# Row maxima in the softmax of a Linformer attention that feeds a SwiGLU block

## The chip, the cores and the metric

The kernel runs on 1 core of one Trainium2 chip. The metric is the device time of one execution in microseconds (us). Engines are named as in the profile: PE is TensorE's matmul, PEld its weight load, DVE is VectorE, ACT is ScalarE, POOL is GpSimd, SP is SyncE. Each engine works off its own queue in order; an instruction that waits holds up everything behind it on its engine.

## The reference

Attention with projected keys and values (8 batches, 8 heads, 1024 positions, head width 64, 64 projected positions), then a gated feed-forward block over the 8192 tokens (512 wide, 1536 hidden).

```
k_proj = einsum('ks,bhsd->bhkd', E, k);  v_proj = einsum('ks,bhsd->bhkd', F, v)
scores = (1/sqrt(64)) * q @ k_proj^T                  # rows of 64
scores = scores - max(scores, axis=-1)
attn = exp(scores);  attn = attn / (sum(attn, -1) + 1e-9)
x = attn @ v_proj, as 8192 x 512
out = (silu(x @ w_gate) * (x @ w_val)) @ w_out
```

## The kernel before

**Work and order.** The kernel is recorded in an order written out by hand; each engine executes its part of it in that order. The main loop runs over t = 0 to 191: 16 chunks c of 512 tokens (two to a batch) times 12 blocks f of 128 hidden columns. In step t, `f_g` puts four matmuls of 512 columns into a PSUM bank `gps`, and ACT takes the tanh of it into `th` (line 496). `f_v` does the same with the other weight into `vps`; DVE then forms `s1 = (th + 1) * g` (line 503) and `hT = 0.5 * s1 * v` (line 508). There are two `gps` and two `vps` banks, so the matmuls of step t+2 wait for the DVE instructions of step t. A PE that has nothing to wait for takes about 0.87 us for each set of four.

The second product of the block (with w_out) lags by one chunk. It is a Strassen-like form with seven products for each half of the chunk (`f_m`, six matmuls of 256 columns at a time, n = 0 to 13 over a chunk at f = 0, 1, 2, 3, 4, 4, 5, 6, 7, 8, 9, 10, 10, 11). ACT copies two of its PSUM results out (`xs`, line 603, at f = 1 and 7; `ysb`, line 610, at f = 3 and 9). The matmuls of n = 2 write the bank that the `xs` copy after n = 1 reads. For chunk 0 the plain form `f_y` is used, during steps 16 to 27.

**Attention.** It is fed in by slots; step t runs slot 2t between its `f_g` and its `f_v`, and slot 2t+1 at its end. A softmax unit u (8 to a batch, 64 in all) holds 128 rows of 8 score rows of 64: `u_S` makes four matmuls of 128 columns into a bank `sc`, and ACT takes one exponential over all 512 columns, with the scale 1/8 in it, into `ee` (line 357). `u_R`, one slot later, sums `ee` on DVE into `zz` (line 368, 128x8 from 128x512) and takes the reciprocals (line 370); `u_N` multiplies on POOL (line 383). For chunk 0 and 1 the result is turned by PE (`u_A`), for the others by a DMA on SP's queue (`u_AD`); `u_PV`, `u_PV1`, `u_PV2` or `u_PVt` multiply with the projected values and ACT or DVE copies the result into `xT`, which `f_g` and `f_v` read. `u_KV`, `u_K1` project keys and values, `u_KT`, `u_KT0` put the projected keys into the block matrix `BD`; ACT copies the keys out (lines 171 and 194). Score banks come from a ring: three banks while c < 2, two afterwards.

**Where the units stand.** Batch 0's units 0 to 3 (chunk 0) are computed before the loop, written out one call after the other (lines 776 to 819); there the first half of the tokens needs units 0 and 2, the second half units 1 and 3. Units 4 to 7 are in slots 13 to 16. The units of batch 1 are in slots 35 to 38 and 41 to 44, close together. Batch 2 has them in slots 48 + (17, 18, 22, 23, 27, 30, 33, 36), and each batch b from 3 on in slots 48(b-1) + (14, 17, 20, 23, 26, 29, 32, 35), one in three slots.

Of the kernel before, what the change touches and what calls it, by code (L numbers as in the profile page):

```python
# [10 lines left out]
ALU = mybir.AluOpType  # L11
# [27 lines left out]
def kernel(  # L39
# [110 lines left out]
    def copy(eng, out, in_):  # L150
        (nc.scalar.copy if eng is nc.scalar else eng.tensor_copy)(out=out, in_=in_)

    def u_KV(b, what="kv", hs=(0, H), at="a"):

# [15 lines left out]
        if "k" in what:  # L170
            nc.scalar.copy(out=ks[b % 2][0:64, h0:h1], in_=t[0:64, h0:h1])
        if "v" in what:
# [7 lines left out]
    def u_K1(b, gs=(0, 2), at="a"):  # L180
# [4 lines left out]
        for j in range(NJ):  # L185
            for c in range(2):
# [6 lines left out]
                )  # L193
        nc.scalar.copy(out=ksp[b][:, 2 * g0 : 2 * g1], in_=t[:])

# [115 lines left out]

    def u_T(b, u, at="a", eng=nc.scalar):
# [10 lines left out]
        t = first_batch("q", [P, 4, P], "qT")  # L323
        copy(eng, t[:], ps[:])
        qT[b, u] = t

# [15 lines left out]

    def u_S(b, u, at="a"):
        ch, w = divmod(u, 4)
# [6 lines left out]
        for n in range(4):  # L351
            slot = (0, 2, 1, 3)[n] if (b, ch) in BY_DMA else n
            nc.tensor.matmul(  # L353
                out=ps[:, slot, :], lhsT=t[:, n, :], rhs=BD[b % 2][:, 4 * g + n, :], start=True, stop=True
            )
        e = aw.tile([P, 4, 2, KP], FP32, name="ee", tag="ee", bufs=4)
        nc.scalar.activation(  # L357
            out=e[:].rearrange("p h j k -> p (h j k)"),
            in_=ps[:].rearrange("p a k -> p (a k)"),
            func=AF.Exp,  # L360
            scale=scale,
        )
        ee[b, u] = e

    def u_R(b, u):
        e = ee[b, u]
        z = aw.tile([P, 4, 2], FP32, name="zz", tag="zz", bufs=3)
        nc.vector.reduce_sum(out=z[:], in_=e[:], axis=AX.X)  # L368
        r = aw.tile([P, 4, 2], FP32, name="rr", tag="rr", bufs=4)
        nc.vector.reciprocal(out=r[:], in_=z[:])  # L370
        rr[b, u] = r

    def u_N(b, u, eng=nc.gpsimd):
# [6 lines left out]
        else:  # L380
# [3 lines left out]
            out=a.rearrange("p j h k -> p h j k"),  # L384
            in0=ee.pop((b, u))[:],
            in1=rr.pop((b, u))[:].unsqueeze(3).to_broadcast([P, 4, 2, KP]),
# [294 lines left out]
    def place(b):  # L681
        s0 = 48 * (b - 1)
        if b == 1:
# [4 lines left out]
            sa = (35, 36, 37, 38, 41, 42, 43, 44)  # L688
            put(41, u_AD, 1, 0)
            put(30, u_TD, 1, 1)  # L690
            put(47, u_AD, 1, 1)
            put(46, u_PVt, 1, 0, (0, 1), ("aa", "av"))
        else:
# [6 lines left out]
            put(s0 + (11 if b == 2 else -4), u_TD, b, 1)  # L700
            sa = [s0 + j for j in ((17, 18, 22, 23, 27, 30, 33, 36) if b == 2 else (14, 17, 20, 23, 26, 29, 32, 35))]
            put(sa[3] + 4, u_AD, b, 0)
            put(sa[7] + 4, u_AD, b, 1)
            put(s0 + 44, u_PVt, b, 0, (0, 1), ("aa", "yz"))
        for j in range(NJ):
            put(sa[j], u_S, b, j)
            put(sa[j] + 1, u_R, b, j)
            put(sa[j] + 1, u_N, b, j)
        put(s0 + (68 if b == 1 else 56), u_PVt, b, 1, (0, 1), ("aa", "yz"))
# [5 lines left out]
    with tc.manual_schedule():  # L715
# [204 lines left out]
```

## Time and profile before

| | |
|---|---|
| median of 3 runs | 546.73 us (546.72 to 546.77) |
| profiled execution, its own time | 546.79 us |
| its span in the profile | 545.0 us (1.8 us of its time lie around it) |
| PE busy | 534.2 us, 98% of the span, clock granted in full |
| DVE busy | 412.8 us, 76% |
| ACT busy | 232.8 us, 43% |
| POOL busy | 294.2 us, 54% |
| exponentials, line 357 | 64 of 595 ns mean |
| sums, line 368 | 64 of 676 ns mean |
| reciprocals, line 370 | 64 of 203 ns mean |

The span is the profile's own clock, from the first instruction to the last. A matmul's duration is modelled with its pipeline, so its mean (379 ns for 512 columns) is longer than the distance between two of them (0.86 us for four). Busy shares are averages over a start of some 22 us, in which the first softmax units are made, and a long main loop.

### The profile page before, as it was taken

Reading aid. Unit: us, or ns where it says so; the run is one execution under the profiler, and the core shown is the slowest. Engines: PE = TensorE matmul, PEld = TensorE weight load, DVE = VectorE, ACT = ScalarE, POOL = GpSimd, SP = SyncE. Lnnn points to the kernel's source line nnn. Section 1 sums busy time; section 2 is a strip of 40 time slices with the busy share of each in tenths; the row PEclk is TensorE's granted clock in tenths of the full one; section 3 lists DMA queues with packets and bytes.
Section 4 is the critical chain, followed back from the end, with each engine's and each line's share of the span. In section 5 each row is a group of like instructions: output and inputs, shape, how many; then the busy total and the mean of one; then the engine's idle time right before and its main releaser. Section 6 shows DMA issues by size and latency. Waiting matters only on the chain.

```text
span 545.0 us, 9374 instructions
## 1 busy us (share of the span) xinstructions
PE 534.2 (98%) x3494; PEld 313.4 (58%) x3556; DVE 412.8 (76%) x697; ACT 232.8 (43%) x416; POOL 294.2 (54%) x364
## 2 busy tenths in 40 slices
PE   8999999999999999999999999999999999999997
PEld 4654445556556555566565665566655665556565
DVE  3787897779668876789777886787967888676884
ACT  3664453354444434444434444434344433443331
POOL 6952393477616854177631865248660655426162
PEclk9999999999999999999999999999999999999999
DMA  9999989929921599008981199512992133110013
GB/s 202 192 196 191 159 155 187 180 75 160 201 68 40 102 186 215 12 30 146 198 160 38 40 144 209 113 40 55 180 206 64 39 78 79 38 40 12 28 40 118
DMA packets 111631, 62.88 MB, mean 115 GB/s; under 512 B 65888, under 2 KB 102752, under 8 KB 111584
## 3 DMA queue, kind: packets, MB, share of 16 engines
q0 software_dynamic: 43952, 29.49, 38.1%
q1 hardware_dynamic: 66800, 31.20, 27.0%
q10 hardware_dynamic: 832, 1.57, 0.9%
q8 instruction: 28, 0.46, 0.3%
q14 instruction: 19, 0.16, 0.1%
HBM read 60.29 MB, written 16.78 MB: 141 GB/s over the span
## 4 chain that ended last, share of the span: by engine, by line
PE 88%; DMA 8%; POOL 2%; issue 1%; ACT 0%; DVE 0%; POOLq 0%; DVEq 0%; ACTq 0%
PE vps L484 28%; PE gps L484 27%; PE yps L586 25%; DMA qTd<-qb 3%; PE sc L353 3%; DMA qb<-in_q_dram 2%; PE kvp L163 2%; DMA Fraw<-in_F_dram 1%; PE pv L430 1%; PE yps L520 1%; DMA wv<-in_moe_w_val_dram 1%; POOL wv L127 0%; POOL AA L383 0%; POOL wg L127 0%; POOL qb L117 0%
## 5 line engine op out<-in xcount | busy, mean ns | idle before, releaser
L496 ACT ACTIVATE th<-gps 128x512 f32<-128x512 f32 x191 | 114.0, 597 | 198.8 <-PE gps L484 178.1
L484 PE MATMUL vps<-xT,wv 128*128 128x512 bf16 (+1 forms) x754 | 195.3, 377 | 0.9
L484 PE MATMUL gps<-xT,wg 128*128 128x512 bf16 (+1 forms) x734 | 192.4, 377 | 1.4
L503 DVE SCALAR_TENSOR_TENSOR s<-th,gps 128x512 f32<-128x512 f32 x191 | 129.2, 677 | 61.5 <-ACT th L496 60.3
L508 DVE SCALAR_TENSOR_TENSOR hT<-s,vps 128x512 bf16<-128x512 f32 x192 | 132.0, 688 | 21.6 <-PE vps L484 1.5
L569 POOL TENSOR_TENSOR hs<-hT 128x256 bf16<-128x256 bf16 x180 | 120.3, 692 | 49.5 <-DVE hT L508 49.5
L484 PEld LDWEIGHTS <-wv 128*128 128x128 bf16 x776 | 73.1, 98 | 85.0 <-issue 6.7
L586 PEld LDWEIGHTS <-hs 128*128 128x128 bf16 x900 | 88.1, 98 | 34.6 <-issue 0.6
L484 PEld LDWEIGHTS <-wg 128*128 128x128 bf16 x776 | 74.0, 98 | 51.7 <-DMA wg<-in_moe_w_gate_dram 0.3
L616 POOL TENSOR_TENSOR tt<-tt,ysb 128x512 f32<-128x512 f32 x28 | 35.6, 1270 | 109.6 <-DVE tt L615 109.6
L383 POOL TENSOR_TENSOR AAd<-ee,rr 128x512 bf16<-128x512 f32 x56 | 58.4, 1044 | 33.6 <-DVE rr L370 32.3
L586 PE MATMUL yps<-ws,hs 128*128 128x256 bf16 x540 | 68.6, 273 | 0.2 <-DVE ysb L653 0.2
L357 ACT ACTIVATE ee<-sc 128x512 f32<-128x512 f32 x64 | 37.9, 595 | 31.9 <-PE sc L353 30.6
L605 POOL TENSOR_TENSOR tt<-xs 128x256 f32<-128x256 f32 x30 | 29.5, 985 | 38.3 <-ACT xs L603 37.7
L586 PE MATMUL yps<-ws,hT 128*128 128x256 bf16 x360 | 48.8, 273 | 0.3
L586 PE MATMUL yps<-wo,hs 128*128 128x256 bf16 x360 | 48.6, 273 | 0.1
L368 DVE TENSOR_REDUCE zz<-ee 128x8 f32<-128x512 f32 x64 | 43.2, 676 | 5.2 <-ACT ee L357 5.1
L569 DVE TENSOR_TENSOR hs<-hT 128x1536 bf16<-128x1536 bf16 (+1 forms) x49 | 45.2, 928 | 0.1
L586 PEld LDWEIGHTS <-hT 128*128 128x128 bf16 x360 | 35.2, 98 | 16.0
L603 ACT COPY xs<-yps 128x512 f32<-128x512 f32 x30 | 17.6, 585 | 28.0 <-PE yps L586 24.7
L610 ACT COPY ysb<-yps 128x512 f32<-128x512 f32 x30 | 17.6, 585 | 27.5 <-PE yps L586 26.6
L439 ACT CAST xT<-pv 128x512 bf16<-128x512 f32 x56 | 28.7, 600 | 0.0
(100 smaller groups left out, 306.0 us busy)
## 6 DMA issues: line engine op xcount, KB each, us to landing
out_dram<-ysb SPq DMA_DIRECT2D x28, 512.0 KB, 2.7
qb<-in_q_dram POOLq DMA_DIRECT2D x14, 512.0 KB, 18.4
kb<-in_k_dram POOLq DMA_DIRECT2D x7, 1024.0 KB, 10.6
vb<-in_v_dram POOLq DMA_DIRECT2D x7, 1024.0 KB, 15.6
wo<-in_moe_w_out_dram POOLq DMA_DIRECT2D x2, 768.0 KB, 21.8
out_dram<-ysb SPq DMA_DIRECT2D x6, 256.0 KB, 2.4
kraw<-in_k_dram ACTq DMA_DIRECT2D x2, 512.0 KB, 4.8
qb<-in_q_dram POOLq DMA_DIRECT2D x4, 256.0 KB, 7.9
```

What stands on the lines that cost most here:

```text
L357: nc.scalar.activation(out=e[:].rearrange("p h j k -> p (h j k)"), in_=ps[:].rearrange("p a k -> p (a k)"), func=AF.Exp, scale=scale,)
L368: nc.vector.reduce_sum(out=z[:], in_=e[:], axis=AX.X)
L383: eng.tensor_tensor(out=a.rearrange("p j h k -> p h j k"), in0=ee.pop((b, u))[:], in1=rr.pop((b, u))[:].unsqueeze(3).to_broadcast([P, 4, 2 ...
L439: nc.scalar.copy(out=xT[b, ch][:, kt, :], in_=ps[:])
L484: nc.tensor.matmul(out=ps[:, ts], lhsT=(wg, wv)[w][:, kt, f * P : (f + 1) * P], rhs=x[:, kt, ts], start=(kt == 0), stop=(kt == NKT - 1),)
L496: nc.scalar.activation(out=th[:], in_=ps[:], func=AF.Tanh, scale=0.5)
L503: nc.vector.scalar_tensor_tensor(out=s1[:], in0=th[:], scalar=1.0, in1=g[:], op0=ALU.add, op1=ALU.mult)
L508: nc.vector.scalar_tensor_tensor(out=hT[c][:, f, :], in0=s1[:], scalar=0.5, in1=ps[:], op0=ALU.mult, op1=ALU.mult)
L569: eng.tensor_tensor(out=hs[c, m][:, fs, :], in0=quarter(hT[c], *a)[:, fs], in1=quarter(hT[c], *b)[:, fs], op=op,)
L586: nc.tensor.matmul(out=ps, lhsT=lhsT, rhs=ws[m][:, f, :] if rhs is None else rhs, start=(start and f == 0), stop=(f == HF - 1), skip_group ...
L605: nc.gpsimd.tensor_tensor(out=t[:, 0], in0=xs[:, 0], in1=xs[:, 1], op=ALU.add)
L616: nc.gpsimd.tensor_tensor(out=t[:], in0=t[:], in1=yo[c, p][:, 1:3], op=ALU.subtract)
```

## The change

In every unit, DVE takes the negated maximum of each score row from PSUM (`nm`, 128x8). The scale 1/8 moves into the copy of the projected keys (`scaled`, an ACT activation with Copy and a scale in place of a copy), so the exponential takes none. Then there are two ways:

- `way="act"` (60 of the 64 units): ACT takes the exponential in eight pieces of 128x64, one for each score row, each with its column of `nm` as a bias and with its sum written to a column of `zz`. DVE's sum over `ee` falls away.
- `way="dve"` (units 0 and 3, 5 and 7 of batch 0): DVE adds `nm` to the scores into `ee` (128x512), ACT takes one exponential in place, and DVE sums as before.

The exponentials become a step of their own, `u_E`, one slot after `u_S`; `u_R` and `u_N` come three slots after `u_S`, two later than before. `zz` has four buffers, it had three. In the part before the loop and in slots 12 to 22 the order is written anew. In batch 1 three steps move by one slot; in batch 2 the units stand in slots 48 + (17, 22, 23, 25, 28, 31, 34, 37); batch 3's loads move four slots later.

```diff
+    def scaled(out, in_):
+        nc.scalar.activation(out=out, in_=in_, func=AF.Copy, scale=scale)
...
-            nc.scalar.copy(out=ks[b % 2][0:64, h0:h1], in_=t[0:64, h0:h1])
+            scaled(ks[b % 2][0:64, h0:h1], t[0:64, h0:h1])
...
-        nc.scalar.copy(out=ksp[b][:, 2 * g0 : 2 * g1], in_=t[:])
+        scaled(ksp[b][:, 2 * g0 : 2 * g1], t[:])
...
-    def u_S(b, u, at="a"):
+    def u_S(b, u, at="a", way="act"):
...
+        m = aw.tile([P, 4, 2], FP32, name="nm", tag="nm", bufs=4)
+        s = ps[:].rearrange("p a (j k) -> p a j k", j=2)
+        nc.vector.tensor_reduce(out=m[:], in_=s, axis=AX.X, op=ALU.max, negate=True)
         e = aw.tile([P, 4, 2, KP], FP32, name="ee", tag="ee", bufs=4)
-        nc.scalar.activation(
-            out=e[:].rearrange("p h j k -> p (h j k)"),
-            in_=ps[:].rearrange("p a k -> p (a k)"),
-            func=AF.Exp,
-            scale=scale,
-        )
-        ee[b, u] = e
+        if way == "dve":
+            nc.vector.tensor_tensor(
+                out=e[:], in0=s, in1=m[:].unsqueeze(3).to_broadcast([P, 4, 2, KP]), op=ALU.add
+            )
+        ee[b, u] = (way, e, m, s)
+
+    def u_E(b, u):
+
+        way, e, m, s = ee[b, u]
+        z = aw.tile([P, 4, 2], FP32, name="zz", tag="zz", bufs=4)
+        if way == "dve":
+            flat = e[:].rearrange("p h j k -> p (h j k)")
+            nc.scalar.activation(out=flat, in_=flat, func=AF.Exp)
+        else:
+            for h in range(4):
+                for j in range(2):
+                    nc.scalar.activation(
+                        out=e[:, h, j, :],
+                        in_=s[:, h, j, :],
+                        func=AF.Exp,
+                        bias=m[:, h, j : j + 1],
+                        accum_out=z[:, h, j : j + 1],
+                    )
+        ee[b, u] = (way, e, z)
...
-        nc.vector.reduce_sum(out=z[:], in_=e[:], axis=AX.X)
+        way, e, z = ee[b, u]
+        if way == "dve":
+            nc.vector.reduce_sum(out=z[:], in_=e[:], axis=AX.X)
...
-            put(41, u_AD, 1, 0)
+            put(42, u_AD, 1, 0)
...
-            put(47, u_AD, 1, 1)
-            put(46, u_PVt, 1, 0, (0, 1), ("aa", "av"))
+            put(48, u_AD, 1, 1)
+            put(47, u_PVt, 1, 0, (0, 1), ("aa", "av"))
...
-            sa = [s0 + j for j in ((17, 18, 22, 23, 27, 30, 33, 36) if b == 2 else (14, 17, 20, 23, 26, 29, 32, 35))]
+            sa = [s0 + j for j in ((17, 22, 23, 25, 28, 31, 34, 37) if b == 2 else (14, 17, 20, 23, 26, 29, 32, 35))]
...
-            put(sa[j] + 1, u_R, b, j)
-            put(sa[j] + 1, u_N, b, j)
+            put(sa[j] + 1, u_E, b, j)
+            put(sa[j] + 3, u_R, b, j)
+            put(sa[j] + 3, u_N, b, j)
...
-        u_S(0, 0, "g")
-        u_R(0, 0)
-        u_N(0, 0)
+        u_S(0, 0, "g", "dve")
...
         u_KV(0, "k", (4, 8), at="y")
+        u_E(0, 0)
         turn(1, "a", (0,), dve)
         u_KT0((2, 4), "vg", (dve, dve, act, act))
-        u_T(0, 1, "a", dve)
-        u_T(0, 3, "a", dve)
+        u_R(0, 0)
+        u_N(0, 0)
+        turned = [u_T(0, u, "a", dve, later=True) for u in (1, 3)]
         turn(1, "a", (1,))
         u_S(0, 2, "g")
-        u_R(0, 2)
-        u_N(0, 2)
+        for done in turned:
+            done()
+        u_E(0, 2)
         u_S(0, 1, "g")
-        u_R(0, 1)
-        u_N(0, 1)
+        u_S(0, 3, "v", "dve")
         load_w_gv(2, 3, (1,))
-        u_S(0, 3, "v")
-        u_R(0, 3)
         load_w_gv(3, 5)
         u_A(0, 0, act)
         u_V0w(0, 2, "y")
         u_V0(2, 3, "v")
         u_PV2(0, 0, 0, 0, act)
+        u_R(0, 2)
+        u_N(0, 2, dve)
         u_A(0, 2, dve)
-        u_N(0, 3, dve)
         u_V0(3, 4, "y")
-        u_PV1(0, 0, 2, 0, act)
-        u_PV1(0, 0, 3, 0, act)
-        u_A(0, 1, act)
+        u_E(0, 3)
+        u_PV1(0, 0, 2, 0, dve)
+        u_PV1(0, 0, 3, 0, dve)
+        u_E(0, 1)
         f_mm(0, 0, 0, 0)
-        u_A(0, 3, dve)
         f_mm(0, 0, 1, 0)
-        u_PV2(0, 0, 0, 1, act)
+        u_R(0, 3)
+        u_N(0, 3)
+        u_R(0, 1)
+        u_N(0, 1, dve)
+        u_A(0, 3, act)
         u_PV1(0, 0, 2, 1, dve)
         u_PV1(0, 0, 3, 1, dve)
         f_mm(0, 1, 0, 0)
         f_mm(0, 1, 1, 0)
+        u_A(0, 1, dve)
+        u_PV2(0, 0, 0, 1, act)
...
-            put(13 + i, u_S, 0, u)
-            put(14 + i, u_R, 0, u)
-            put(14 + i, u_N, 0, u)
-            put((17, 18, 20, 21)[i], u_A, 0, u, nc.scalar)
-        put(19, u_PV, 0, 1, 0)
+            put(13 + i, u_S, 0, u, "a", ("act", "dve")[i % 2])
+            put(14 + i, u_E, 0, u)
+            put(16 + i, u_R, 0, u)
+            put(16 + i, u_N, 0, u)
+            put(18 + i, u_A, 0, u, nc.scalar)
+        put(20, u_PV, 0, 1, 0)
...
-            s0 = 48 * (b - 1) - (20 if b == 3 else 24)
+            s0 = 48 * (b - 1) - (16 if b == 3 else 24)
```

More of the change, by code (lines that the diff above doesn't have):

```diff
@@ L310, in first_batch, with u_T @@
         return hs_tile(ms[n % len(ms)], shape, name)
-    def u_T(b, u, at="a", eng=nc.scalar):
+    def u_T(b, u, at="a", eng=nc.scalar, later=False):
         ch, w = divmod(u, 4)
@@ L323, in u_T @@
         t = first_batch("q", [P, 4, P], "qT")
+        qT[b, u] = t
+        if later:
+            return lambda: copy(eng, t[:], ps[:])
         copy(eng, t[:], ps[:])
-        qT[b, u] = t
     def u_TD(b, ch):
@@ L355, in u_S @@
             )
+        m = aw.tile([P, 4, 2], FP32, name="nm", tag="nm", bufs=4)
+        s = ps[:].rearrange("p a (j k) -> p a j k", j=2)
+        nc.vector.tensor_reduce(out=m[:], in_=s, axis=AX.X, op=ALU.max, negate=True)
         e = aw.tile([P, 4, 2, KP], FP32, name="ee", tag="ee", bufs=4)
-        nc.scalar.activation(
-            out=e[:].rearrange("p h j k -> p (h j k)"),
-            in_=ps[:].rearrange("p a k -> p (a k)"),
-            func=AF.Exp,
-            scale=scale,
-        )
-        ee[b, u] = e
+        if way == "dve":
[20 more added lines that the diff above has]
+        ee[b, u] = (way, e, z)
     def u_R(b, u):
-        e = ee[b, u]
-        z = aw.tile([P, 4, 2], FP32, name="zz", tag="zz", bufs=3)
-        nc.vector.reduce_sum(out=z[:], in_=e[:], axis=AX.X)
+        way, e, z = ee[b, u]
+        if way == "dve":
+            nc.vector.reduce_sum(out=z[:], in_=e[:], axis=AX.X)
         r = aw.tile([P, 4, 2], FP32, name="rr", tag="rr", bufs=4)
@@ L384, in u_N @@
             out=a.rearrange("p j h k -> p h j k"),
-            in0=ee.pop((b, u))[:],
+            in0=ee.pop((b, u))[1][:],
             in1=rr.pop((b, u))[:].unsqueeze(3).to_broadcast([P, 4, 2, KP]),
```

## The prediction

> **What bounds the kernel now.** First I read the head of the profile and its 40 slices.
>
> ```profile
> span 545.0 us, 9374 instructions
> PE 534.2 (98%) x3494; PEld 313.4 (58%) x3556; DVE 412.8 (76%) x697; ACT 232.8 (43%) x416; POOL 294.2 (54%) x364
> PE   8999999999999999999999999999999999999997
> ACT  3664453354444434444434444434344433443331
> ```
>
> PE is busy in every slice but the start and the end, and the clock row has a 9 throughout. PE's work is not touched, so little can be won: a gain could only come out of the 545.0 - 534.2 = 10.8 us that PE idles, mostly before 22 us. A loss comes wherever a score bank, a tanh or `xT` is late by more than its slack. ACT looks free at 43%, but that is an average, so next I read ACT's rows in the groups and the timeline.
>
> ```profile
> L357 ACT ACTIVATE ee<-sc 128x512 f32<-128x512 f32 x64 | 37.9, 595 | 31.9 <-PE sc L353 30.6
> L368 DVE TENSOR_REDUCE zz<-ee 128x8 f32<-128x512 f32 x64 | 43.2, 676 | 5.2 <-ACT ee L357 5.1
> ...
> 14.85 1.58 ACT L357 ACTIVATE ee<-sc 128x512 f32<-128x512 f32 x3
> 16.91 0.54 ACT L244 CAST BDV<-kvp 64x128 bf16<-64x128 f32 x2
> 18.94 0.66 ACT L151 CAST xT<-pv 128x256 bf16<-128x256 f32 x2
> ...
> 271.86 2.05 ACT L439 CAST xT<-pv 128x512 bf16<-128x512 f32 x4
> ```
>
> Three exponentials in a row take 1.58 us, so one starts each 0.49 us. Two copies of only 128 columns take 0.54, so one starts each 0.27: a quarter of the columns costs over half the time. Durations say the same: 585 ns for 512 columns, 372 for 256, 262 for 128, about 0.83 ns a column and some 0.16 us that stay. The last view is the timeline at the start and in batch 1.
>
> ```profile
> 20.84 0.58 ACT L151 CAST xT<-pv 128x512 bf16<-128x512 f32 x1 [0.75 <-PE pv L447]
> 22.15 0.60 PE L484 MATMUL gps<-xT,wg 128*128 128x256 bf16 x4
> 45.25 1.03 PE L484 MATMUL gps<-xT,wg 128*128 128x512 bf16 x4
> 61.24 0.60 ACT L496 ACTIVATE th<-gps 128x512 f32<-128x512 f32 x1 [0.21 <-PE gps L484]
> 78.58 0.60 ACT L496 ACTIVATE th<-gps 128x512 f32<-128x512 f32 x1 [1.73 <-PE gps L484]
> 79.15 2.05 ACT L439 CAST xT<-pv 128x512 bf16<-128x512 f32 x4
> 81.63 1.03 PE L484 MATMUL gps<-xT,wg 128*128 128x512 bf16 x4
> ```
>
> These are the deadlines: second-half matmuls at 22.15, chunk 1 at 45.25, chunk 2 at 81.63, each right behind ACT's copy to `xT`.
>
> **The cost of a unit on ACT, U.** An "act" unit was one instruction and becomes eight, each with a bias column and a sum that is written out; no row has either. From below: eight small instructions at the distance of the 128-column pair, 8 x 0.27 = 2.2 us, bias and sum free. Still lower, if they overlap as wide ones do (512 columns last 0.60 and start 0.49 apart): 0.16 + 0.05 - 0.11 = 0.10 each, 0.8 us. From above: the sum is a second small instruction behind each piece, 8 x 0.54 = 4.3. I take the middle of 2.2 and 4.3, U = 3.2 us (0.40 a piece), against 0.49 before. The trace has no ACT instruction started under 0.27 behind another small one, so 0.8 is far.
>
> The Trainium skill ("ScalarE: Activation LUTs", section "What ACT_TABLE_LOAD costs") has a rule that speaks against the change: a bias by pointer adds about 93 ns, so an ACTIVATE takes 280 ns + 0.833 ns a column, and neighbours overlap by 93 ns. An estimate from that page is 333 - 93 = 240 ns a piece, U = 1.9, under the 0.27 of the trace's pair, and it gives no price for the sum; by it the total below would be about 553 us.
>
> **DVE.** Per "act" unit a maximum from PSUM comes (512 elements in, 128x8 out) and a sum from SBUF goes. PSUM as a source makes no difference in the rows (L503 677 ns from PSUM, L368 676 from SBUF), so DVE's 76% stays: about zero, hidden under PE. The four "dve" units keep the sum and add a maximum and an addition, 4 x 1.35 = 5.4 us, off PE's path but for the start. The scaled key copies cost what copies cost (595 against 597 ns for an activation with a scale): nothing.
>
> **Where the time shows**, stage by stage, with ACT's queue in its new order.
>
> *Start (units 0 to 3).* Scores of unit 2 are ready at 14.85, where its exponential ran. Now DVE first copies `BD`, sums unit 0 and takes its reciprocal (to 15.15), then takes the maximum to 15.9. Pieces of unit 2: 15.95 to 19.15. Behind them in ACT's queue stand a copy to `AT`, three to `BDV`, one to `xT` and unit 3's exponential (some 3.0 us with a short wait for PE), then unit 1's pieces, 22.15 to 25.35. Then reciprocal and multiply on DVE (0.9), two `xT` copies there (0.8), turning on PE, copy 0.4, PV, and the `xT` copy 0.6 on ACT: 29.15 where the trace has 22.15. That is +7.0 us, in general 2U + 0.6. The weights that POOL queues behind unit 3's multiply are late by some 5 us, less than PE itself.
>
> *Units 4 to 7.* ACT's queue is now pieces of 4 from 35.1, a `qT` copy, 5, tanh, pieces of 6, 7: with U = 3.2, 43.7 at the end of unit 7. Sum 0.68, reciprocal 0.2, POOL's multiply 1.04, turning 1.0, PV 0.3 and copy 0.69 with their hand-overs lead to 47.9 for chunk 1, where it was 45.25: +2.65 (2U - 3.75).
>
> *Batch 1.* From the end of tanh 18 at 61.84, ACT's queue holds, with nothing for it to wait for, eight units, five tanh at 0.5, two `ysb` copies at 0.5, then another and the four copies to `xT` (2.55): 61.84 + 8U + 3.5 + 2.55 = 93.5 against 81.63 for chunk 2: +11.85 (8U - 13.75). Eight exponentials took 4 us in these 17 us; now they need 25.6, and a PE that would run ahead is held by the two `gps` banks, each waiting for a tanh behind pieces.
>
> *Batch 2.* Units stand after tanh 35, 36, 37 with the `xs` copy of f = 1 behind them: from the end of matmul set 35, 0.6 + 3U + 1.5 = 11.7 us until `xs` is out, and n = 2 wants that bank at 8.6: +3.1 (3U - 6.5).
>
> *Batches 3 to 7.* One unit in 1.5 steps. A step is 2 x 0.87 + 0.65 = 2.39 us, with scores (0.22) and the doubled `f_m` at f = 4 and 10 a mean of 2.65; so 3.97 us hold U + 1.5 x 0.5 + 0.25 for copies = 4.2: ACT is over its share, and lags. A tanh may end some 2.3 us late (its DVE instruction takes 0.7, the second set after begins 3.9 us behind its own). Walking the queue (pieces, tanh, tanh, pieces, `ysb`, tanh, pieces ...) with U = 3.2, sets 10, 13, 16 and 19 wait 0.05, 0.15, 0.6 and 0.3: +1.1 a batch, 5.5 in all. With U = 3.0 the walk gives none, with 3.4 it gives 2.4; beyond 3.03 about 6.5 us per us of U and batch.
>
> New waits: DVE's maximum waits for scores with the step's `s1` behind it, but `s1` waits 0.7 us for its tanh anyway. Reciprocals come two slots later and so after their pieces. POOL's multiplies and SP's transposes move with them; in batch 1 the transpose is done by about 85, before the 93 that ACT sets. Batch 3's loads come 4 slots (5 us) later on POOL's queue; its transposes on SP's, now some 148 to 155, still end before the first scores at 168, and outputs queued there have two buffers. If that cover were gone, it would cost those 5 us once.
>
> **The sum**: 7.0 + 2.65 + 11.85 + 3.1 + 5.5 = 30.1 on the execution's own 546.8 (span 545.0 and 1.8 around it; the median is 546.7): 577 us.
>
> **Rivals.**
> *Cheap pieces*: bias and sum free, U = 2.2. The small pair speaks for it; against it, that a result of its own must be written. Start 5.0, units 4 to 7 0.65, batch 1 3.85, batch 2 0.1, later none: 9.6, 556.4 us.
> *Double pieces*: U = 4.3, ACT becomes the bound wherever units stand. Start 9.2, then 4.85, 20.65, 6.4 and 5 x 8.25: 82.4, 629 us. The distance of small instructions speaks for it, the overlap of wide ones against.
> *Not slower*: pieces overlap to 0.10 us (U = 0.8), so ACT keeps all its slack; the start's formula then leaves 2.2 us (549.0), and the time is that of before, 547, only if that too falls into PE's waits there, which decides from 1.1 us of the start upward. In its favour are 10 us of idle PE; against it, that no small ACT pair runs like that and that unit 2 and 1 both wait for DVE's new step.
>
> **How the numbers follow.** Forecast (U from 2.6 to 3.8, 562 to 605): 0.56. Cheap pieces, or in between, 0.22. Double pieces and beyond 605, 0.19. Not slower 0.03. The likeliest gives 577. The range drops the cheapest third of the cheap and the dear half of the double cases: from U = 2.2, 556, to 3.95, 612. A measurement tells 0.2% (1.1 us) from no change; faster 0.02, same 0.01, slower 0.97.
>
> **What would show it.** The pieces' row: 480 of them (60 x 8), and the time from one unit's first to its last, 3.2 us; ACT's busy share near 233 + 60 x 2.7 = 395 us, 69% of the span; second-half matmuls near 29, chunk 1 some 9.7 later than before, chunk 2 some 21.5 later, then 1 us a batch; PE's idle time charged to tanh and its DVE instruction. It is wrong if DVE rather than ACT holds the banks (its maximum slower than 0.7 us, or its queue late behind waits), or if a piece lies outside 0.27 to 0.54 us.

## The result and the profile after

| | before | after |
|---|---|---|
| median of 4 runs each, side by side | 546.74 us (546.72 to 546.77) | 599.09 us (598.38 to 599.18) |
| profiled execution, own time | 546.79 us | 599.16 us |
| span | 545.0 us | 597.4 us |

The kernel became slower: the ratio is 1.0955, with a 95% interval of 1.0936 to 1.0974. The forecast was 577 us with a range of 556 to 612. Head and slices of the changed kernel:

```profile
span 597.4 us, 10325 instructions
PE 551.6 (92%) x3556; PEld 317.3 (53%) x3556; DVE 416.8 (70%) x708; ACT 336.6 (56%) x1314; POOL 290.9 (49%) x363
PE   7688996999899998999899998999989998999997
ACT  3556388259744666447754486447664477643331
PEclk9898998999989999999999999999999999999999
```

Now the groups, with busy time, mean ns, and the idle time before the instruction and who ended it:

```profile
L528 DVE SCALAR_TENSOR_TENSOR s<-th,gps 128x512 f32<-128x512 f32 x191 | 131.0, 686 | 89.4 <-ACT th L521 88.3
L381 ACT ACTIVATE ee<-sc,nm 128x64 f32<-128x64 f32 x480 | 144.2, 343 | 39.9 <-DVE nm L363 38.1
...
L381 ACT ACTIVATION_READ_ACCUMULATOR ee<-sc,nm 128x1 f32 x480 | 110.5, 235 | 0.0
...
L611 PE MATMUL yps<-ws,hs 128*128 128x256 bf16 x540 | 68.6, 272 | 18.8 <-DVE tt L640 18.7
...
L363 DVE TENSOR_REDUCE nm<-sc 128x8 f32<-128x512 f32 x64 | 41.8, 656 | 3.3 <-PE sc L358 3.3
...
L395 DVE RECIPROCAL rr<-zz 128x8 f32<-128x8 f32 x64 | 12.5, 198 | 24.2 <-ACT ee L381 24.0
```

What the reader is to see: ACT's busy share rose from 43% to 56%, so no engine but PE is near its limit; DVE fell from 76% to 70%. The 480 pieces are each two instructions, an exponential (343 ns) and a read-out of its sum (235 ns), overlapped. But ACT waits 38.1 us for the maxima, DVE waits 24.0 us for the pieces at its reciprocals, and PE waits 18.7 us for a DVE instruction on line 640 that has nothing to do with the softmax. Before, DVE waited 5.1 us for exponentials, at its sums; the other two waits were not there.

Line 640 belongs to the second product: it reads a PSUM bank of one Strassen product out, and PE's products n = 6 and n = 13 write that bank next. It stands in DVE's queue behind `s1`, which waits for a tanh. The next view, the changed kernel's timeline in a steady batch (start, duration, instruction; in brackets the idle time before and who ended it), follows one unit into the next and ends with the matmuls that wait; the chain below it shows what led up to them.

```profile
354.92 0.20 DVE L395 RECIPROCAL rr<-zz 128x8 f32<-128x8 f32 x1 [1.16 <-ACT ee L381]
355.03 0.64 DVE L363 TENSOR_REDUCE nm<-sc 128x8 f32<-128x512 f32 x1
...
355.77 0.32 ACT L381 ACTIVATE ee<-sc,nm 128x64 f32<-128x64 f32 x1
...
356.86 0.39 PE L358 MATMUL sc<-BD,qTd 128*128 128x128 bf16 x4
...
358.11 1.12 ACT L521 ACTIVATE th<-gps 128x512 f32<-128x512 f32 x2
...
358.77 0.69 DVE L528 SCALAR_TENSOR_TENSOR s<-th,gps 128x512 f32<-128x512 f32 x1 [0.85 <-ACT th L521]
...
359.57 0.69 DVE L533 SCALAR_TENSOR_TENSOR hT<-s,vps 128x512 bf16<-128x512 f32 x1
360.17 0.95 DVE L594 TENSOR_TENSOR hs<-hT 128x1536 bf16<-128x1536 bf16 x1
...
361.04 0.20 DVE L395 RECIPROCAL rr<-zz 128x8 f32<-128x8 f32 x1
361.15 0.64 DVE L363 TENSOR_REDUCE nm<-sc 128x8 f32<-128x512 f32 x1
...
361.89 0.32 ACT L381 ACTIVATE ee<-sc,nm 128x64 f32<-128x64 f32 x1 [2.66 <-DVE nm L363]
...
367.24 0.82 PE L611 MATMUL yps<-ws,hs 128*128 128x256 bf16 x6 [2.58 <-DVE tt L640]
```

```profile
362.97 1.40 ACT ee L381 x9
364.37 0.47 ACT ysb L635
364.85 0.51 ACT th L521
365.38 0.70 DVE s L528
366.23 0.54 issue
366.78 0.43 DVE tt L640
367.24 0.82 PE yps L611 x6
```

It is a loop between two queues. Pieces run from 355.77 to 358.11 (2.34 us). They hold up two tanh on ACT. So `s1` on DVE starts at 358.77, after 0.85 us of idling, and behind it in DVE's queue stand `hT`, a sum of `hT` blocks, a reciprocal and then the next unit's maximum. Its scores were made at 356.86, but the maximum starts only at 361.15. So the next pieces start at 361.89, after ACT has idled 2.66 us with them at the head of its queue and the next tanh behind them. When this shift reaches a step in which line 640 is due, PE waits: 2.58 us before the matmuls at 367.24.

**Where the time went.** The table below is worked out from the traces: the start of the `hT` instruction of step t (line 508 before, 533 after), less the same in the kernel before, as increase from stage to stage. Example: step 24 started at 84.12 before and 105.12 after, 21.0 us later; step 12 was 12.6 later, so the stage in between lost 8.4. The prediction's terms stand beside it.

| stage | predicted | measured |
|---|---|---|
| start, up to step 0 | 7.0 | 7.0 |
| chunk 0 (steps 0 to 12), units 4 to 7 | 2.65 | 5.6 |
| chunk 1 (12 to 24), batch 1's units | 11.85 | 8.4 |
| chunks 2 and 3 (24 to 48), batch 2's units | 3.1 | 7.6 |
| steps 48 to 168, batches 3 to 7 | 5.5 | 23.8 (three times 4.1, twice 5.8) |
| sum | 30.1 | 52.4 |

### The profile page after: what moved, and what is told of

Same layout as the page of the kernel before. It is cut to its first block, busy times and chain, and to the rows that moved or that the text cites. A ratio compares the mean times of both kernels' runs of the same rounds, so it can differ in the third digit from the quotient of the medians.

```text
span 597.4 us, 10325 instructions
## 1 busy us (share of the span) xinstructions
PE 551.6 (92%) x3556; PEld 317.3 (53%) x3556; DVE 416.8 (70%) x708; ACT 336.6 (56%) x1314; POOL 290.9 (49%) x363
## 4 chain that ended last, share of the span: by engine, by line
PE 75%; ACT 13%; DVE 7%; issue 2%; DMA 1%; POOL 1%; DVEq 0%; POOLq 0%; ACTq 0%
PE gps L509 24%; PE vps L509 24%; PE yps L611 20%; ACT ee L381 10%; PE kvp L166 2%; DVE s L528 2%; PE sc L358 2%; ACT th L521 1%; DVE nm L363 1%; DMA Fraw<-in_F_dram 1%; PE pv L455 1%; DVE hT L533 1%; ACT ysb L635 1%; DVE tt L640 1%; PE yps L545 0%
## 5 line engine op out<-in xcount | busy, mean ns | idle before, releaser
L509 PE MATMUL gps<-xT,wg 128*128 128x512 bf16 (+1 forms) x772 | 200.8, 383 | 3.2 <-ACT xT L464 2.5
L521 ACT ACTIVATE th<-gps 128x512 f32<-128x512 f32 x191 | 116.6, 617 | 154.5 <-PE gps L509 154.1
L509 PE MATMUL vps<-xT,wv 128*128 128x512 bf16 (+1 forms) x776 | 202.1, 384 | 0.0
L528 DVE SCALAR_TENSOR_TENSOR s<-th,gps 128x512 f32<-128x512 f32 x191 | 131.0, 686 | 89.4 <-ACT th L521 88.3
L381 ACT ACTIVATE ee<-sc,nm 128x64 f32<-128x64 f32 x480 | 144.2, 343 | 39.9 <-DVE nm L363 38.1
L509 PEld LDWEIGHTS <-wv 128*128 128x128 bf16 x776 | 74.6, 99 | 88.3 <-issue 11.9
L381 ACT ACTIVATION_READ_ACCUMULATOR ee<-sc,nm 128x1 f32 x480 | 110.5, 235 | 0.0
L641 POOL TENSOR_TENSOR tt<-tt,ysb 128x512 f32<-128x512 f32 x28 | 35.6, 1270 | 103.7 <-DVE tt L640 103.7
L611 PE MATMUL yps<-ws,hs 128*128 128x256 bf16 x540 | 68.6, 272 | 18.8 <-DVE tt L640 18.7
L630 POOL TENSOR_TENSOR tt<-xs 128x256 f32<-128x256 f32 x30 | 26.9, 899 | 38.8 <-ACT xs L628 38.4
L363 DVE TENSOR_REDUCE nm<-sc 128x8 f32<-128x512 f32 x64 | 41.8, 656 | 3.3 <-PE sc L358 3.3
L628 ACT COPY xs<-yps 128x512 f32<-128x512 f32 x30 | 18.1, 604 | 21.9 <-PE yps L611 16.1
L395 DVE RECIPROCAL rr<-zz 128x8 f32<-128x8 f32 x64 | 12.5, 198 | 24.2 <-ACT ee L381 24.0
## 6 DMA issues: line engine op xcount, KB each, us to landing
kb<-in_k_dram POOLq DMA_DIRECT2D x7, 1024.0 KB, 10.3
```

What stands on the lines that cost most here:

```text
L363: nc.vector.tensor_reduce(out=m[:], in_=s, axis=AX.X, op=ALU.max, negate=True)
L381: nc.scalar.activation(out=e[:, h, j, :], in_=s[:, h, j, :], func=AF.Exp, bias=m[:, h, j : j + 1], accum_out=z[:, h, j : j + 1],)
L509: nc.tensor.matmul(out=ps[:, ts], lhsT=(wg, wv)[w][:, kt, f * P : (f + 1) * P], rhs=x[:, kt, ts], start=(kt == 0), stop=(kt == NKT - 1),)
L521: nc.scalar.activation(out=th[:], in_=ps[:], func=AF.Tanh, scale=0.5)
L528: nc.vector.scalar_tensor_tensor(out=s1[:], in0=th[:], scalar=1.0, in1=g[:], op0=ALU.add, op1=ALU.mult)
L611: nc.tensor.matmul(out=ps, lhsT=lhsT, rhs=ws[m][:, f, :] if rhs is None else rhs, start=(start and f == 0), stop=(f == HF - 1), skip_group ...
```

## The experiments

Three theories were set against each other. **A, length of the pieces:** ACT has more work per unit and lags, as the prediction had it. **B, the coupling:** a unit's pieces wait for a maximum that waits in DVE's queue behind work which waits for ACT; each part alone would cost little. **C, the bank of line 640** has too little slack, and taking the product later would give the time back. Each kernel is the changed one with the edit shown. The summary, in us; the stages are worked out as above, from each kernel's profile. The changed kernel and the last two were timed in four executions each, the others in one. Beside them the kernel before took 546.4 to 546.9.

| kernel | time | start | chunk 0 | chunk 1 | 24 to 48 | 48 to 168 |
|---|---|---|---|---|---|---|
| changed kernel | 599.1 | 7.0 | 5.6 | 8.4 | 7.6 | 23.8 |
| bias of zeros, maximum kept | 600.1 | 8.4 | 7.1 | 8.3 | 7.6 | 21.8 |
| pieces without sums | 588.4 | 6.3 | 5.4 | 3.1 | 3.8 | 23.2 |
| one exponential, maximum unused | 572.7 | 6.4 | 5.4 | 2.8 | 2.6 | 8.7 |
| n = 6 a step later | 592.6 | 6.9 | 5.6 | 8.3 | 8.1 | 17.0 |
| pieces, no maximum | 564.5 | 4.8 | 3.7 | 5.3 | 2.5 | 1.4 |
| new order alone | 557.7 | 5.6 | 1.5 | 2.4 | 1.0 | 0.4 |
| exponentials a slot later | 581.6 | 6.4 | 5.6 | 8.4 | 7.6 | 6.9 |
| all units the "dve" way | 616.9 | 10.3 | 8.8 | 7.6 | 7.4 | 36.0 |
| later, and spread in batches 1 and 2 | 578.1 | 6.8 | 5.6 | 3.8 | 8.2 | 6.9 |
| common maximum, one exponential | 573.2 | 6.4 | 5.4 | 2.2 | 3.2 | 9.0 |
| common maximum, spread, start reordered | 568.7 | 6.8 | 3.5 | 2.5 | 4.4 | 7.2 |
| put together from the best stages | 563.5 | 5.8 | 2.7 | 1.7 | 2.6 | 4.0 |

### A bias of zeros in place of the maxima

```diff
+    zb = const.tile([P, 1], FP32, name="zb")
...
+        nc.gpsimd.memset(zb[:], 0.0)
...
-                        bias=m[:, h, j : j + 1],
+                        bias=zb[:],
```

> The pieces take a column of zeros as their bias; the maxima are still taken on DVE, in the same place, but nothing reads them, so no row's maximum is taken out. Pieces, sums, and the order of every queue stay. Theory A (the prediction's: the length of the pieces on ACT, 2.3 us a unit, sets the loss): about the time of the changed kernel, 595 to 600 us. Theory B (the pieces wait for DVE's maximum, which stands behind an s1 that waits for a tanh that stands behind the previous unit's pieces): the 38 us in which ACT idles for nm are gone, pieces start 1 to 2.6 us earlier, and the time falls to 570 to 585 us.

600.13 us: nothing gained. The waits of this kernel say why it separates nothing (us in total, times, longest us):

```profile
ACT ee L382 <- DVE nm L364: 38.6, 25, 2.7
```

The pieces no longer use `nm`, and still wait for the instruction that writes it, as often and as long as before the edit (38.1, 25, 2.7). Both read the score bank, and in this program the second reader still waits for the first. So the wait was still in the kernel, and this run speaks neither for A nor for B. It shows that where the bias comes from is of no account for the time.

### The sums back on DVE

```diff
-                        accum_out=z[:, h, j : j + 1],
...
-        if way == "dve":
+        if True:
             nc.vector.reduce_sum(out=z[:], in_=e[:], axis=AX.X)
```

> The pieces give no sum; DVE sums ee in all units, as before the change (64 sums of some 0.68 us instead of 4). Theory A: without the read-out of the accumulator, a unit's pieces take 1.6 to 2.0 us in place of 2.3, ACT's work falls by 20 to 40 us, and 20 us or more of the loss go: 570 to 580. Theory B: DVE gets 40 us more work in the queue that the pieces wait for, so little is won or it gets worse: 590 to 610.

588.42 us. Without a sum there is no read-out, and eight pieces take 1.75 us from first start to last end, where they took 2.34. In this kernel's timeline, and its group row:

```profile
336.23 1.75 ACT L381 ACTIVATE ee<-sc,nm 128x64 f32<-128x64 f32 x8 [0.58 <-DVE nm L363]
...
351.46 1.75 ACT L381 ACTIVATE ee<-sc,nm 128x64 f32<-128x64 f32 x8 [3.31 <-DVE nm L363]
```

```profile
L381 ACT ACTIVATE ee<-sc,nm 128x64 f32<-128x64 f32 x480 | 105.3, 344 | 60.1 <-DVE nm L363 60.0
```

ACT was busy 295.1 us in place of 336.6, 41.5 less. The dense batch 1 gained from it (3.1 in place of 8.4), but the later batches, where units stand three slots apart, lost 23.2 as before (23.8): what the pieces gave up, the sums took on DVE (453.2 us busy, it was 416.8), and ACT's wait for maxima grew to 60.0 us. Under A the later batches should have recovered. That counts against it there, not in batch 1.

### One exponential, the maximum taken but unused

```diff
-            for h in range(4):
-                for j in range(2):
-                    nc.scalar.activation(
...
+            nc.scalar.activation(out=e[:], in_=s, func=AF.Exp)
...
-        if way == "dve":
+        if True:
             nc.vector.reduce_sum(out=z[:], in_=e[:], axis=AX.X)
```

In the 60 units concerned, the maximum is not subtracted.

> One exponential over 512 columns without a bias and DVE's sum, as before the change; the maxima are still taken on DVE but not used, so no row's maximum is taken out. Slots and queues are those of the changed kernel. If the eight pieces are the cause (A and B alike), the time is near that of before: 548 to 553, with the start 1 to 3 us later because of DVE's maximum. If the new order or DVE's 43 us of maxima are the cause: above 570.

572.74 us, not the 548 to 553 that A and B alike had led to. It is still 26.2 above the kernel before, which ran beside it (546.54), with ACT at 230.2 us, less than before the change. What is left is the order and the maximum, for which ACT waits 50.9 us:

```profile
L379 ACT ACTIVATE ee<-sc 128x512 f32<-128x512 f32 x60 | 35.8, 599 | 53.1 <-DVE nm L363 50.9
```

### The product n = 6 one step later

```diff
-for n, f in enumerate((0, 1, 2, 3, 4, 4, 5, 6, 7, 8, 9, 10, 10, 11)):
+for n, f in enumerate((0, 1, 2, 3, 4, 4, 6, 6, 7, 8, 9, 10, 10, 11)):
```

> The product n = 6 of the first half of a chunk moves from step f = 5 to f = 6, so that its matmuls give DVE (line 640) one step more to read the bank they write. Theory C (that bank is the deadline that the late tanh breaks: PE waits 18.7 us for line 640, 10 times): the waits of 2.6 us at f = 5 go, five batches give back 2 to 2.6 us each, 585 to 590. Theory A: the same lateness is met at the next bank, 596 to 600.

592.58 us, 6.5 less. PE's waits in this kernel:

```profile
PE yps L611 <- ACT xs L628: 6.6, 7, 2.9
PE gps L509 <- DVE s L528: 6.1, 5, 1.2
PE yps L611 <- DVE tt L640: 5.6, 5, 1.1
```

The wait for line 640 fell from 18.7 to 5.6 us, but two others took 6.6 and 6.1; before the edit the first was 3.2 and the second not in the list. So the bank of line 640 is only where the lateness arrives first (C in part): with that door open, PE goes on until the tanh itself, through `s1` and the `gps` bank, holds it.

### Pieces without a maximum, and the order alone

The first of these takes no maximum (zeros as a bias, pieces and sums as in the changed kernel); the second does the arithmetic of the kernel before (one exponential, sums on DVE, no maximum) in the new order and slots. Neither subtracts the maxima.

```diff
-        nc.vector.tensor_reduce(out=m[:], in_=s, axis=AX.X, op=ALU.max, negate=True)
...
-                        bias=m[:, h, j : j + 1],
+                        bias=zb[:],
```

> No maximum is taken at all (the pieces have zeros as bias, the four dve units one exponential straight from PSUM), so ACT waits for the scores alone; pieces, sums and order stay. Theory A (pieces on ACT set the loss): 590 or more. Theory B (the wait for DVE's maximum sets it; in e1 the built program still waited for DVE, since both engines read the same bank): 565 to 580, ACT's 38 us of waits for nm gone.

```diff
-        nc.vector.tensor_reduce(out=m[:], in_=s, axis=AX.X, op=ALU.max, negate=True)
...
-            for h in range(4):
-                for j in range(2):
-                    nc.scalar.activation(
...
+            nc.scalar.activation(out=e[:], in_=s, func=AF.Exp)
...
-        if way == "dve":
+        if True:
             nc.vector.reduce_sum(out=z[:], in_=e[:], axis=AX.X)
```

> The arithmetic of before (no maximum, one exponential, DVE's sum in all units) in the slots and the order of the changed kernel. If the new order costs nothing: 547 to 549. If the loss that e3 still has (26 us, of it 11.7 before chunk 1) comes from the order and the later reciprocals: 560 or more. If from DVE's maximum and the wait for it: under 550.

564.46 us, just under the 565 to 580 expected of B, and 557.68 us, between the two expectations; each ran beside 546.39. With the two runs above this makes a square; each figure is a time less that of the kernel before beside it:

| | no maximum | maximum on DVE |
|---|---|---|
| one exponential, DVE sums | +11.3 | +26.2 |
| eight pieces with sums | +18.1 | +52.4 |

The order costs 11.3, pieces add 6.8 to it, a maximum adds 14.9; if they were independent, both would make 33.0. The changed kernel loses 52.4: 19.4 us come only when the two are together (some of it through PE's clock, see the last section). From step 48 on it is plainer still: 0.4, 1.4, 8.7 and 23.8. In the kernel without a maximum, ACT has the same pieces, and its rows are

```profile
L376 ACT ACTIVATE ee<-sc,zb 128x64 f32<-128x64 f32 x480 | 144.6, 369 | 0.0
L376 ACT ACTIVATION_READ_ACCUMULATOR ee<-sc,zb 128x1 f32 x480 | 119.3, 264 | 0.0
```

with no idle time before them, ACT 59% busy, and no wait for the read-out of line 640 (line 635 in that kernel) in the list of PE's waits. A falls for the later batches: the same length of pieces, 1.4 us lost. It keeps a share in batch 1, where eight units stand close (5.3 against 2.4 for the order alone).

### Exponentials one slot later

```diff
-            put(sa[3] + 4, u_AD, b, 0)
-            put(sa[7] + 4, u_AD, b, 1)
+            put(sa[3] + 5, u_AD, b, 0)
+            put(sa[7] + 5, u_AD, b, 1)
...
-            put(sa[j] + 1, u_E, b, j)
-            put(sa[j] + 3, u_R, b, j)
-            put(sa[j] + 3, u_N, b, j)
+            later = 1 if b > 1 else 0
+            put(sa[j] + 1 + later, u_E, b, j)
+            put(sa[j] + 3 + later, u_R, b, j)
+            put(sa[j] + 3 + later, u_N, b, j)
```

> From batch 2 on the exponentials, reciprocals, multiplies and transposes come one slot later, so that in half the units a tanh stands ahead of the pieces that wait for DVE. Theory B: ACT does the tanh while it waits, PE's waits for line 640 shrink, 575 to 590 us. Theory A: the sum of the work on ACT is the same, 597 to 601.

581.64 us, with every instruction of the changed kernel in it. Its waits:

```profile
ACT ee L381 <- DVE nm L363: 6.0, 8, 2.7
...
PE yps L611 <- DVE tt L640: 4.7, 11, 0.5
...
DVE rr L395 <- ACT ee L381: 2.7, 6, 1.3
```

ACT's wait for maxima fell from 38.1 to 6.0 us, DVE's wait for pieces from 24.0 to 2.7, PE's for line 640 from 18.7 to 4.7, and the later batches lose 6.9 in place of 23.8. Chunks 2 and 3, where batch 2's exponentials moved too, still lose 7.6. No work was taken away: the loop was only given another slot of room, and in half the units a tanh now goes ahead of the pieces. For batches 3 to 7 this is the direct test of B. The edit moves the exponential and the reciprocal behind it together, so which of the two links mattered more is not shown; moving one alone was not tried.

### Every unit by way of DVE

```diff
-    def u_S(b, u, at="a", way="act"):
+    def u_S(b, u, at="a", way="dve"):
...
-            put(13 + i, u_S, 0, u, "a", ("act", "dve")[i % 2])
+            put(13 + i, u_S, 0, u, "a", "dve")
```

> All units the other way: DVE adds the negated maximum (0.69 us) and sums (0.68), ACT takes one exponential. ACT is as before the change, DVE has 1.37 us a unit more than in the changed kernel, 82 us in all, near 84% of the span. If ACT's pieces are the larger cost: 575 to 590. If DVE's queue is (B): 595 to 620, since the scores wait for two DVE passes.

616.91 us, the slowest. ACT is down to 38% (230.9 us) and DVE up to 80%:

```profile
ACT ee L377 <- DVE ee L366: 103.0, 51, 5.2
```

ACT's free time helps nothing: with 1.37 us more on DVE in each unit (the expectation's figure), ACT waits 103.0 us for the additions, and the later batches lose 36.0 in place of 23.8.

### One maximum for eight rows

```diff
+            m = aw.tile([P, 1], FP32, name="nm", tag="nm1", bufs=4)
+            nc.vector.tensor_reduce(
+                out=m[:], in_=ps[:].rearrange("p a k -> p (a k)"), axis=AX.X, op=ALU.max, negate=True
+            )
...
+            nc.scalar.activation(out=e[:], in_=s, func=AF.Exp, bias=m[:])
...
-        if way == "dve":
+        if True:
             nc.vector.reduce_sum(out=z[:], in_=e[:], axis=AX.X)
```

One maximum for the eight rows of a partition shifts all eight alike, so the weights are still those of a softmax; it isn't each row's own maximum.

> One maximum over all eight rows of a partition (128x1) in place of eight, used as the bias of a single exponential of 512 columns; DVE sums every unit. The weights stay those of a softmax. Order as in the changed kernel. If the bias operand and the wait for the maximum are dear by themselves, it stays near the changed kernel: 590 or more. If the maximum costs by its place in DVE's queue and the pieces by their coupling with it, it takes what the run with one exponential and an unused maximum took, 572.7, within 2 us: 571 to 575.

573.23 us, 0.5 from the run with an unused maximum (572.74). Using the result as a bias costs the kernel no more than having to wait for it. The rows of this kernel:

```profile
L385 ACT ACTIVATE ee<-sc,nm 128x512 f32<-128x512 f32 x60 | 41.2, 688 | 53.3 <-DVE nm L367 51.2
...
L367 DVE TENSOR_REDUCE nm<-sc 128x1 f32<-128x512 f32 x60 | 39.1, 652 | 1.8 <-PE sc L358 1.7
```

### Later and spread

```diff
-            sa = (35, 36, 37, 38, 41, 42, 43, 44)
+            sa = (35, 36, 37, 38, 41, 43, 48, 51)
...
-            put(48, u_AD, 1, 1)
+            put(56, u_AD, 1, 1)
...
-            sa = [s0 + j for j in ((17, 22, 23, 25, 28, 31, 34, 37) if b == 2 else (14, 17, 20, 23, 26, 29, 32, 35))]
+            sa = [s0 + j for j in ((17, 20, 23, 26, 29, 32, 35, 38) if b == 2 else (14, 17, 20, 23, 26, 29, 32, 35))]
...
+            later = 1 if b > 1 or j > 3 else 0
```

> Exponentials one slot later again, now also for units 4 to 7 of batch 1; besides, those units stand in slots 41, 43, 48, 51 in place of 41 to 44, batch 2's units three slots apart from its slot 17 on, and from batch 2 on the transposes stand right behind the last multiply. If the loss comes from one unit's pieces meeting the next unit's maximum (the coupling), it is dear where units stand close together: with exponentials later alone, chunk 1 to 2 lost 8.4 us, chunk 2 to 4 lost 7.6, each later batch 1.15. Then chunk 2 to 4 should fall to about 2 us and the later batches to 0.3 to 0.6, and chunk 1 to 2 by 1 to 2 us since its first four units are still dense: 570 to 574 us. If the amount of work on ACT sets the loss, spreading it moves nothing but the place: 579 to 584.

578.13 us, between the two expectations. Chunk 1 lost 3.8 in place of 8.4, more gained than expected; but steps 24 to 48 lost 8.2 where 2 had been expected, and the later batches kept 1.2 each (from batch 4 on). PE's waits there are others: 0.72 us for the transposed weights from DMA and 2.18 for the copies to `xT` ahead of chunk 2, 1.85 and 1.65 for pieces and `xT` copies ahead of chunk 3. Part of the loss only moved. What would free chunks 2 and 3 with pieces on ACT is not settled. Wider spacing in batch 1 was tried too: with units 4 to 7 in slots 43, 46, 49 and 52 the recorded order deadlocks (its queues wait for each other in a circle), so it has no time.

### Two versions with the common maximum

The first adds the spreading and the later slots, and makes all units of batch 0 the same way, with the exponentials of units 1 and 3 right behind their scores:

```diff
-        u_S(0, 3, "v", "dve")
+        u_S(0, 3, "v")
+        u_E(0, 1)
+        u_E(0, 3)
...
-            put(13 + i, u_S, 0, u, "a", ("act", "dve")[i % 2])
+            put(13 + i, u_S, 0, u)
```

> The common maximum with a single exponential, sums on DVE, the same spreading and later exponentials, and all units of batch 0 in that way too (the start's order moved to fit: exponentials of units 1 and 3 right behind their scores, their sums before the first matmuls of the main loop). With the common maximum alone the loss was 6.4 us at the start, 5.4 in chunk 0, 2.2 in chunk 1, 3.2 in batch 2 and 1.8 in each later batch: 573.2. If what is left of it is again a unit's exponential waiting behind a late maximum and holding up the tanh, the later batches fall to 0.3 or less, batch 2 to about 1, and the first three to 8 to 13 in all: 555 to 562 us. If DVE's work (79% busy) is the limit by itself, the later batches stay at 1.8 and it ends at 565 to 573.

568.65 us (566.91 to 571.23 in 4 runs), ratio to before 1.039 (1.037 to 1.0413). Its profiled execution, from which its stages are, took 571.2. The later batches lost 0.95 each (batches 4 to 6), where the common maximum alone lost 1.8: half-way between the expectations; the total lies in the range that stood for DVE's work as the limit (565 to 573), above the 555 to 562 of the other. In the trace the rest is a wait of 0.79 us for line 640, once a batch, before n = 6.

The second takes the first's start, batch 1 in the changed kernel's order, later exponentials from batch 2 on, batch 2's second unit two slots earlier than in the changed kernel, and n = 6 one step later:

```diff
-            sa = [s0 + j for j in ((17, 22, 23, 25, 28, 31, 34, 37) if b == 2 else (14, 17, 20, 23, 26, 29, 32, 35))]
+            sa = [s0 + j for j in ((17, 20, 23, 25, 28, 31, 34, 37) if b == 2 else (14, 17, 20, 23, 26, 29, 32, 35))]
...
+            later = 1 if b > 1 else 0
...
-for n, f in enumerate((0, 1, 2, 3, 4, 4, 5, 6, 7, 8, 9, 10, 10, 11)):
+for n, f in enumerate((0, 1, 2, 3, 4, 4, 6, 6, 7, 8, 9, 10, 10, 11)):
```

> Put together from the stages that lost least: the common maximum with the start of the run before it, batch 1 in the changed kernel's order, batch 2 and later with exponentials one slot later, and the product n = 6 one step later. By stages measured in other runs: 6.8 at the start, 3.5 in chunk 0, 2.4 in chunk 1, 2 to 3 in batch 2. If the 0.8 us that each later batch still lost in the run before it is the wait of n = 6 for line 640's instruction alone, the later batches lose nothing: 14.5 to 16 us, 561 to 563. If taking it later only moves that wait to a later matmul set, they keep 0.95 each: 567 to 569.

563.51 us (562.79 to 563.72; 561 to 563 was expected), ratio to before 1.0302 (1.0285 to 1.0319): 35.6 us under the changed kernel, and still slower than before. From step 72 to the end it loses 0.2 us in all. Here n = 6 a step later takes the rest of the wait without making a new one of note: PE's longest wait for `s1` is 0.3 us. Still ACT waits for maxima:

```profile
ACT ee L385 <- DVE nm L367: 19.8, 16, 2.3
```

From step 72 on these waits cost PE next to nothing. The 16.7 us that remain are lost before step 72: 5.8 at the start, 2.7, 1.7 and 2.6 in the next stages, and 3.8 between steps 48 and 72, 2.1 of them one wait for a transpose by DMA.

## Why the prediction was right, and where it was wrong

**Right: the direction, and that it is a matter of queues.** ACT at 56% is free on average, and the kernel lost 9.6%; tanh and its DVE instruction are the messengers, though PE's longest waits are charged to line 640 behind them (18.7 us). 599.1 lies in the range, 22 us above the forecast.

**The size of U.** It was put at 3.2 us between bounds of 2.2 and 4.3; it is 2.34 (355.77 to 358.11; eight pieces 0.29 us apart). The upper bound's picture, the sum as a second small instruction behind each piece, is what the trace has: the read-out of 235 ns. But it overlaps its piece, so the pair takes 0.29 and not 0.54. The 0.27 taken as the distance of small instructions was no floor either: without sums pieces start 0.20 apart, and in the prediction's own lines two copies of 256 columns take 0.66 us, where one lasts 0.37, so they start 0.29 apart, about as far as the two of 128. The 69% expected for ACT became 56%.

**The sum fits for a poor reason.** By the prediction's own formulas U = 2.34 gives 5.3 at the start, 0.9, 5.0 and 0.5 in the next stages and none in the later batches: 11.7 in all, 558.5 us. The U that was too large hid some 18 of the 41 us that the formulas leave out.

**The step that failed** is the pair "so DVE's 76% stays: about zero, hidden under PE" and "`s1` waits 0.7 us for its tanh anyway" for the new wait. As work the first was right (412.8 us busy, then 416.8). But both count what an instruction takes, not what it waits for or what waits behind it. The walk through ACT's queue let each unit's pieces start on time; in the trace they start when DVE has reached the maximum, 25 times late, 38.1 us in all. Without the maximum the later batches lose 1.4 us in place of 23.8, and with one slot more between it and the pieces 6.9. The prediction named this among the things that would make it wrong ("its queue late behind waits") and gave it no price.

**The order had almost no term.** With one exponential a unit (U = 0.49) the formulas give 1.6 us at the start and nothing behind it; the run with the order alone lost 5.6 there, 11.3 in all. The sum also keeps PE at full clock throughout, and the changed kernel's mean granted clock was 0.980.

**"Reciprocals come two slots later and so after their pieces"** was wrong: DVE waited for pieces at 25 of 64 reciprocals, 24.0 us. In a batch with one unit in three slots, the reciprocal of a unit stands right before the next unit's maximum, so this wait is passed straight on to the next pieces.

**Stage by stage.** *Start:* matmuls of the second half at 29.16, predicted 29.15, by luck: unit 2's and 1's pieces were 0.9 us shorter each, and three things came on top: PE waited 1.32 us for unit 3's multiply on POOL, the next two sets ran at half clock (1.06 us each in place of 0.60), and PE waited 0.68, 0.52 and 0.68 us for copies before and behind them. With the old arithmetic in the new order the start lost 5.6 as well, so most of it is the order, not the pieces. *Chunk 0:* 5.6 against 2.65; without a maximum it is 3.7, with the order alone 1.5. *Batch 1:* 8.4 against 11.85, the one stage that was put down too dear; 2.4 of it is order. *Batch 2 and the later ones:* 31.4 where 8.6 had been put down. In the later ones most of it is the coupling; batch 2 lost the same 7.6 with its exponentials a slot later, and what would free it stays open.

**The rivals.** "Cheap pieces" was nearly right about the pieces (2.2 against 2.34) and 43 us off in the time. "Double pieces" (629) had the right idea of a read-out and the wrong length. "Not slower" needed pieces of 0.10 us; they take 0.29, or 0.20 without sums ((1.75 - 0.34) / 7).

## What to carry to other kernels

When a step on one in-order queue now needs a result from another, draw the loop: what stands ahead of the producer, and does any of that wait for the consumer's engine? If it does, its length in waits and hops has to fit into the distance between two such steps, and the queue neighbours of both sides count in full; here one slot of distance was worth 17 us (some 3.4 of them through PE's clock, see below), and pieces a quarter shorter (1.75 us for 2.34, the sums moved to DVE) 11. And two changes made together should be run apart and together: each alone cost 7 and 15 us here, and both 41 above the order.

## What the runs showed of the hardware that was not expected

**A sum from ACT is a second instruction.** 480 read-outs of 235 ns mean stand beside the 480 pieces, and with them the pieces start 0.29 us apart, without sums 0.20.

**A bias by pointer cost 89 ns.** The 512-column exponential took 599 ns without a bias (the run with an unused maximum) and 688 with one, 89 ns more. The Trainium skill ("ScalarE: Activation LUTs", section "What ACT_TABLE_LOAD costs") gives about 93 ns for a bias by pointer, and its formula makes 333 ns of a piece that took 343 here; both agree with these runs.

**PE's clock fell to half after some waits, and not after others.** In the changed kernel's timeline and windows (PE busy, then the other engines, then the granted clock, the third number from the right):

```profile
98.60 0.41 PE L455 MATMUL pv<-AT,VS 64*64 64x512 bf16 x4 [1.96 <-ACT ee L381]
101.51 1.86 PE L509 MATMUL gps<-xT,wg 128*128 128x512 bf16 x4 [2.50 <-ACT xT L464]
```

```profile
23.00:25.00 2.00, 0.55 (x5) 0.39 (x6) 0.90 (x2) 1.35 (x7) 2.00 (x3) 0.94 1.07 143
25.00:27.00 2.00, 2.00 (x11) 1.44 (x10) 0.76 (x2) 0.00 (x0) 2.00 (x4) 0.50 0.88 109
27.00:29.00 2.00, 0.97 (x7) 0.60 (x6) 1.14 (x3) 0.48 (x1) 2.00 (x4) 0.71 1.48 186
...
298.00:300.00 2.00, 2.00 (x6) 0.73 (x5) 1.90 (x5) 0.60 (x1) 0.04 (x1) 0.50 1.30 184
...
368.00:370.00 2.00, 2.00 (x15) 1.04 (x13) 1.64 (x3) 0.82 (x2) 0.61 (x1) 1.00 1.21 194
```

Four matmuls that take 1.03 us take 1.86 after the two gaps before chunk 2, and in the start, after gaps of 1.32 and 0.68 us, the clock is at half for some 3.4 us (0.94, 0.50 and 0.71 in three windows). So a wait on PE can cost more than its length: the two sets at 101.51 and 103.17 alone lost some 1.7 us (1.86 and 1.91 against 1.03). But a gap does not decide it alone. Of the five waits of 2.58 us for line 640, the two that end at 296.61 and 505.14 were followed by half clock for about 3.4 us, the other three, 367.24 among them, by full clock. Those two lie in the two later batches that lost 5.8 us; the other three lost 4.1. The Trainium skill ("TensorE: Matmul & The Clock Gate", section "What's actually happening") has the clock halve after an idle window of about 3.4 us that runs freely; here neither gap before chunk 2 reached that, and PE worked 0.4 us between them. What decides it is not shown here.

How much of the loss this is can be estimated from the mean granted clock, 1.000 before and 0.980 after: at most 2% of 597.4 us, 11.9 us, since PE idled in a part of it. The other three kernels of the square have 0.993 (order alone), 0.996 (pieces) and 0.990 (maximum), which makes 3.9, 2.3 and 5.7 us, so by this estimate some 8 of the 19.4 us are clock. It does not overturn the reading: in the later batches half clock cost 3.4 of the 23.8 us (1.7 in each of two batches), and the runs with n = 6 or the exponentials later, which had no half clock from step 48 on, gained 6.8 and 16.9 there, 3.4 of it clock each time.
